# Which step TensorE is handed next: a planner's rule for heads and feed-forward, and the rings of its PSUM banks

## The chip, the cores and the metric

One core of a Trainium2 chip runs the whole program. The time is that of one execution on the device, in microseconds (us); of several runs the median counts. The engines are PE (TensorE, matrix products), DVE (VectorE), ACT (ScalarE), POOL (GpSimd) and SP (SyncE, here a queue of DMA issues). PE writes to PSUM, which has eight banks; each holds 128 x 512 floats.

## The reference

For 8 batches, 8 heads, 576 positions and a head width of 64, block-causal attention is computed; its heads are put side by side to rows of 512; then comes a mixing by a two-dimensional Fourier transform, a normalization and a feed-forward layer of width 2048:

```python
scores = scale * np.matmul(q, k.transpose(0, 1, 3, 2))
scores = np.where(block_i >= block_j, scores, -1000000000.0)   # blocks of 64 positions
attn = softmax(scores)                                          # written out in the reference
x = np.matmul(attn, v)                                          # heads joined: (8, 576, 512)
mixed = np.real(fft(fft(x, axis=1), axis=2))
u = x + mixed
un = (u - mu) / np.sqrt(var + 1e-06)                            # over the 512 of a row
out = u + np.maximum(un @ w_ch1, 0.0) @ w_ch2
```

## The kernel before

**The work.** Products are made of 16-bit halves: each operand is split into a high and a low part, and three of the four cross products are added up. A head (64 of them) goes through PE in stages: four pieces of row maxima (`max_part`, matmuls named ps<-lead with 72 rows; DVE reduces them to M), one `shift` (a transpose of the maxima, ps<-ident,M; ACT makes mt of it, and a DMA of SP's queue writes it into row 72 of "lead"), four pieces of scores (`scores`, ps<-rest and ps<-lead with 73 rows; ACT takes the exponential twice, POOL subtracts to get the low part "pl"), and five steps of values (`values`, av<-VH,ph and the like). These are 14 steps for a head. Two heads share loads and splits of q, k and v.

When the eight heads of a batch are done, its transform follows (`fourier_steps`): a gather through DRAM, folds on DVE and ACT, first stages on PE (ps<-dft,fs), second stages (ps<-dft,zs and ps<-dft,zc), sums on POOL. Then rows of 256 are normalized and turned (`normalized_steps`, ps<-ident,un), and each such group becomes one feed-forward job (`feed_steps`): 18 jobs in all, two for batch 0 and two for batch 1. A job has 64 first-layer steps of three matmuls (h<-uh,W and h<-ul,W) and 32 second-layer steps of three (acc<-W,gh and acc<-W,gl). Job 1 does all of its first layer ahead of its second, because the weights are still being split; later jobs interleave the two layers by pairs of 128 columns.

**The planner.** The order of the instructions on every engine is made when the program is built, by a planner at the end of the kernel. It keeps a clock of its own, `now`, which is PE's; a booked time for each engine; the time at which each finished step is expected to be usable (`done`); and for each pool of PSUM banks a list of the times at which its banks come free (`rings`). A `Step` has a PE cost, a chain of what follows it on other engines (A is ACT, D is DVE, G is POOL, Q is SP's queue, M and L the transfer; every hop adds HOP = 0.3 us), and the keys it comes after. Steps stand in lanes: loads, heads, transforms. The feed-forward steps are a lane of their own; its next step is called `filler`, and `feed` says that it may go. `ready(step)` is the time at which a step's inputs, and a bank where it needs one, are expected.

What is taken next is decided here (lines 1315 to 1323, with MARGIN = 0.3 at line 39):

```python
feed = filler is not None and may(filler)
sure = now - (MARGIN if feed and ready(filler) <= now else 0.0)
soon = [i for i in able if ready(heads[i]) <= sure]
if soon:
    i = min(soon, key=lambda i: heads[i].place)
elif feed and ready(filler) <= now or feed and not able:
    i = None                                        # the feed-forward's step
elif able:
    i = min(able, key=lambda i: ready(heads[i]))
```

So with a ready feed-forward step, a step of the other lanes goes first only if it has been ready for 0.3 us. With no ready step at all, the step of the other lanes that is ready first is taken, even where the feed-forward's would be ready before it.

**Banks.** `ps_av` has one bank; `BANKS = {"ps": 3, "h": 2, "acc": 2}` are the other seven. "h" and "acc" belong to the feed-forward jobs; before the first of these, all seven are lent to everything else (`lent`), later the three of "ps" alone. `rings["ps"]` has three times in the order in which the banks were taken, and the one taken longest ago is always the next.

**Order on the chip.** Every engine executes its instructions in the planner's order; semaphores hold an instruction until its inputs are there and until its bank has been read. The planner's expected times have no power over the chip: where a step was expected too early, PE stands and waits.

Of the kernel before, what the change touches and what calls it, by code (L numbers as in the profile page):

```python
# [19 lines left out]
B, H, S, D = 8, 8, 576, 64  # L20
DM = H * D
FF = 4 * DM
P = 128
NF = FF // P
NK = DM // P
# [10 lines left out]


HOP = 0.3
MARGIN = 0.3
AHEAD = (3.0, 6.0)  # L40
FREE = 0.5
BACKLOG = 3.0
# [4 lines left out]

PSHIFT = 5

BANKS = {"ps": 3, "h": 2, "acc": 2}  # L50

KM = D + 8
KS = KM + 1
# [153 lines left out]
def tile_attn_fourier_ffn(  # L207
# [13 lines left out]
    def mm(*args, **kw):  # L221
        return tc.keep_in_program_order(nc.tensor.matmul(*args, **kw))  # L222
# [44 lines left out]
    def both(h):  # L267

        return half_tiles(h % NB)[0:2]
# [33 lines left out]
    lent = list(BANKS)  # L303


    scratch = {"p": [0.0] * 2, "t": [0.0] * 2, "n": [0.0] * 2}

    def may(step):
        return all(x in done for x in step.after) and all(x in done for x in step.need)
# [391 lines left out]
    def values(h, at):  # L701
        g, hh = divmod(h, 2)
        b, n = divmod(h, H)
        vh, vl = VH[g % 2], VL[g % 2]
        if at == 0:
            avs[h] = ps_av.tile([P, 5, D + 1], F32, name="av")
        av = avs[h]
        c = CHUNKS[at]
        tile_, col = ((0, 0), (1, 0), (2, 0), (2, 320), (1, 448))[c]
        ph, pl = probs[h, tile_]  # L710
        for j in range(c, 5):

# [24 lines left out]
        vector.tensor_scalar(den, av[:, :, D], eps, sc, op0=ALU.add, op1=ALU.mult)  # L737
        rec = work.tile([P, 5], F32, name="rec", bufs=2)
        vector.reciprocal(rec, den)
        vector.tensor_tensor(  # L740
            x[:, :, hh], av[:, :, 0:D], rec.unsqueeze(2).to_broadcast([P, 5, D]), op=ALU.mult
        )
        yield
        if hh == 1:
            ds = slice(D * (n - 1), D * (n + 1))
            sync.dma_start(
                xd[0:512, ds].rearrange("(c p) d -> p c d", p=P), x[:, 0:4].rearrange("p c h d -> p c (h d)")
            )
            sync.dma_start(xd[512:576, ds], x[64:128, 4].rearrange("p h d -> p (h d)"))
            yield  # L750
# [31 lines left out]
        return work.tile([P, 2, DM], F32, name="u", bufs=5)  # L782

    def fourier_steps(b):
        U, X, low, up = [], [], [], []

        def mirror():
            xd = xs.pop(b)
            LL, UU = utile(), utile()
            U.extend((UU[:, 0], UU[:, 1], work.tile([97, DM], F32, name="U2", bufs=1)))  # L790
            X.extend((LL[:, 0], LL[:, 1], work.tile([33, DM], F32, name="X2", bufs=1)))
            low.extend(X[0:2])
            up.extend(U[0:2])
            if b % 2 == 0:
                lefts.append(work.tile([P, DM], F32, name="left", bufs=2))
            U2 = U[2]
            sync.dma_start(X[2], xd[256:289])
# [103 lines left out]
        def stage2_cos(c):  # L901
            na, nb = (128, 128) if c < 2 else (33, 32)
            t = ps_tile()
            i = 0
            ns = slice(P * c, P * c + na)
            for m in range(2):
                for a, w in ((0, 0), (0, 1), (1, 0)):
                    mm(t[0:na, 0:KCOL], z["c", m][:, a, ns], cd[:, m, w], start=(i == 0), stop=False)
                    i += 1
            mm(t[0:na, 0:KCOL], ZT[:, ns], tail, start=False, stop=True)  # L910
            yield
            bs = bss[c]
# [115 lines left out]
    def feed_steps(me, uh, ul, us, stores):  # L1028
# [35 lines left out]
        def second(f, n):  # L1064
            if f == 0:
                acc.append(ps["acc"].tile([P, DM], F32, name="acc"))
            gh, gl = gs[f]
            ns = slice(P * n, P * (n + 1))
            for j, (g_, w) in enumerate(((gh, 0), (gh, 1), (gl, 0))):
                mm(acc[n], g_[:, ns], W[:, NF + f, w], start=(f == 0 and j == 0), stop=(f == NF - 1 and j == 2))  # L1070
            if f == NF - 1:
                yield
                u = us[n]
                vector.scalar_tensor_tensor(u, acc[n], inv_w, u, op0=ALU.mult, op1=ALU.add)
                yield
                stores[n](u)
                yield

        def first_steps(f):
            for part in range(NK):  # L1080
# [150 lines left out]
    def weight_lane(w):  # L1231
# [11 lines left out]
        for j in range(NF):  # L1243
# [10 lines left out]
                lambda: weight_parts(NF * w + j), 0.0, ("A0.73", "p1", "A0.72", "G1.2", "p") if j % 2 else ("A0.73", "X0.75"), (("scale", w), ("w", NF * w + j - 2)), ("w", NF * w + j),  # L1254
            )

    def store(b, c):
        return lambda u: sync.dma_start(out[b, P * c:P * (c + 1)], u)

# [27 lines left out]
    while True:  # L1287
# [29 lines left out]
        soon = [i for i in able if ready(heads[i]) <= sure]  # L1317
        if soon:
            i = min(soon, key=lambda i: heads[i].place)
        elif feed and ready(filler) <= now or feed and not able:  # L1320
            i = None
        elif able:
            i = min(able, key=lambda i: ready(heads[i]))
        elif any(sides):
            w = min((w for w, x in enumerate(sides) if x is not None and may(x)), key=lambda w: ready(sides[w]))
            issue(sides[w])
            sides[w] = next(weights[w], None)
            continue
        elif pending:
            give(pending[0][0])  # L1330
            continue
        else:
            assert filler is None and not any(heads)
            break
        if i is None:
            if len(lent) > 1:
                now = max(now, ready(filler), *rings["h"], *rings["acc"])
                lent = ["ps"]
            issue(filler)
            filler = None  # L1340
        else:
            issue(heads[i])
            heads[i] = next(lanes[i], None)
# [46 lines left out]
```

## Time and profile before

| | |
|---|---|
| median of 3 runs | 1216.81 us (1213.17 to 1217.76) |
| the profiled execution | 1216.37 us, its span 1214.6 us |
| PE busy | 1145.7 us, 94% of the span |
| DVE, ACT, POOL busy | 57%, 47%, 34% |
| mean granted clock of TensorE | 0.983 |
| feed-forward matmuls | h 3456 of 256 columns, acc 1728 of 512 columns |

Busy time of PE is the union of its matmuls' spans, whose ends are modelled: it tells whether PE stood idle, not how fast it went. The granted clock is the share of full speed that TensorE was given; at 0.5 a matmul takes twice as long. In a line of the timeline or of a group the tile written stands left of "<-", the tiles read right of it. All instructions go through the helpers at lines 200, 222 and 225, so it is the tiles' names that tell them apart.

### The profile page before, as it was taken

How to read it: one execution, taken by the hardware profiler on the slowest of the kernel's cores; microseconds unless marked ns; L12 is line 12 of the kernel's file. 1: busy time of each engine (PE TensorE's matmuls, PEld its weight loads, DVE VectorE, ACT ScalarE, POOL GpSimd, SP SyncE). 2: the span in 40 equal slices, each digit the busy share in tenths (PEclk: the TensorE clock that was granted, in tenths of full speed). 3: DMA queues.
4: the chain of work that ended last, by engine and by line, in shares of the span. 5: the costliest groups of instructions: out<-in, count | busy, mean ns of one | idle time of the engine just before them, and what ended most of it. 6: DMA issues, size and time to landing. Idle time of an engine off the chain costs nothing.

```text
span 1214.6 us, 25361 instructions
## 1 busy us (share of the span) xinstructions
PE 1145.7 (94%) x10122; PEld 818.8 (67%) x10122; DVE 691.0 (57%) x1525; ACT 568.6 (47%) x1269; POOL 417.0 (34%) x507
## 2 busy tenths in 40 slices
PE   5777788998999999999999999999999999999998
PEld 4553475676677777777776776777677767766665
DVE  6877887566857656675555565657454424431211
ACT  5656667755556465445554535645552112111100
POOL 4552625444443544254242452335350400300000
PEclk9998899999799999999999999999999999999999
DMA  8775453333424234133234222423230110000000
GB/s 259 238 230 168 143 131 104 98 101 91 124 60 130 69 100 128 59 105 88 78 100 116 60 78 81 143 57 95 61 82 11 43 38 2 23 18 1 18 18 18
DMA packets 66124, 108.23 MB, mean 89 GB/s; under 512 B 9671, under 2 KB 36209, under 8 KB 66006
## 3 DMA queue, kind: packets, MB, share of 16 engines
q1 hardware_dynamic: 58662, 82.25, 24.1%
q10 hardware_dynamic: 4384, 16.78, 4.2%
q0 software_dynamic: 2960, 7.58, 2.2%
q8 instruction: 80, 1.31, 0.5%
q14 instruction: 38, 0.31, 0.1%
HBM read 58.50 MB, written 18.89 MB: 64 GB/s over the span
## 4 chain that ended last, share of the span: by engine, by line
PE 83%; DVE 6%; DMA 5%; POOL 2%; ACT 2%; issue 2%; SPq 0%; DVEq 0%; ACTq 0%; POOLq 0%
PE acc L222 30%; PE h L222 30%; PE ps L222 15%; PE av L222 6%; DMA lead<-mt 2%; DVE W L200 2%; PE ps L225 1%; DVE M L200 1%; DMA lead<-rest 1%; POOL u L200 1%; DMA u<-in_moe_w_ch_dram 1%; POOL pl L200 1%; DMA V<-in_v_dram 0%; ACT p L200 0%; SPq L200 0%
## 5 line engine op out<-in xcount | busy, mean ns | idle before, releaser
L222 PE MATMUL h<-uh,W 128*128 128x256 f16 x2304 | 433.0, 274 | 0.0
L200 POOL TENSOR_TENSOR pl<-p,ph 128x288 f16<-128x288 f32 (+1 forms) x256 | 260.1, 1028 | 356.7 <-ACT p L200 327.4
L222 PEld LDWEIGHTS <-W 128*128 128x128 f16 x3456 | 332.7, 99 | 63.4 <-issue 1.9
L222 PE MATMUL acc<-W,gh 128*128 128x512 f16 x1104 | 328.8, 379 | 0.0
L222 PE MATMUL h<-ul,W 128*128 128x256 f16 x1152 | 315.2, 274 | 0.0
L222 PE MATMUL acc<-W,gl 128*128 128x512 f16 x552 | 209.3, 379 | 0.0
L200 DVE SCALAR_TENSOR_TENSOR gl<-h,gh 128x512 f16<-128x512 f32 x138 | 94.9, 688 | 199.9 <-ACT gh L200 199.6
L200 ACT ACTIVATE gh<-h 128x512 f16<-128x512 f32 x138 | 82.4, 597 | 264.9 <-PE h L222 264.0
L200 DVE TENSOR_REDUCE M<-ps 128x1 fp32r<-128x320 f32 (+3 forms) x293 | 131.0, 483 | 119.2 <-PE ps L222 119.0
L222 PE MATMUL ps<-lead 73*128 73x288 f16 (+7 forms) x708 | 162.8, 293 | 16.7 <-DMA lead<-in_c_masks_dram 6.7
L200 ACT ACTIVATE ph<-ps 128x288 f16<-128x288 f32 (+1 forms) x235 | 119.0, 508 | 99.1 <-PE ps L222 98.2
L222 PEld LDWEIGHTS <-gh 128*128 128x128 f16 x1104 | 102.6, 98 | 83.5 <-issue 3.9
L222 PEld LDWEIGHTS <-ph 128*128 128x128 f16 x1920 | 114.2, 103 | 24.5 <-issue 5.1
L222 PE MATMUL av<-VH,pl 128*128 128x65 f16 x960 | 115.7, 200 | 9.0 <-POOL pl L200 7.0
L200 ACT ACTIVATE p<-ps 128x288 f32<-128x288 f32 (+1 forms) x235 | 118.0, 505 | 2.1 <-POOL pl L200 1.0
L222 PE MATMUL av<-VH,ph 128*128 128x65 f16 x960 | 117.0, 202 | 0.7 <-ACT p L200 0.7
L222 PE MATMUL av<-VL,ph 128*128 128x64 f16 x960 | 116.3, 200 | 0.0
L222 PEld LDWEIGHTS <-pl 128*128 128x128 f16 x960 | 93.8, 102 | 11.2 <-POOL pl L200 8.9
L222 PE MATMUL ps<-rest 128*128 128x320 f16 (+3 forms) x356 | 98.3, 291 | 1.6 <-DVE M L200 1.3
L222 PEld LDWEIGHTS <-gl 128*128 128x128 f16 x552 | 53.8, 97 | 65.6 <-DVE gl L200 0.3
L222 PEld LDWEIGHTS <-lead 73*128 73x128 f16 (+1 forms) x744 | 66.1, 103 | 39.0 <-issue 6.5
L222 PEld LDWEIGHTS <-rest 128*128 128x128 f16 x372 | 38.7, 104 | 30.6 <-issue 11.8
(203 smaller groups left out, 1376.3 us busy)
## 6 DMA issues: line engine op xcount, KB each, us to landing
raw<-in_qk_dram SPq DMA_DIRECT2D x30, 576.0 KB
W<-in_moe_w_ch_dram ACTq DMA_DIRECT2D x14, 1024.0 KB
V<-in_v_dram SPq DMA_DIRECT2D x32, 320.0 KB
rest<-lead SPq DMA_DIRECT2D x64, 144.0 KB
rest<-rest SPq DMA_DIRECT2D x60, 144.0 KB
out_dram<-u SPq DMA_DIRECT2D x32, 256.0 KB
xd<-x SPq DMA_DIRECT2D x30, 256.0 KB
lead<-lead SPq DMA_DIRECT2D x60, 72.0 KB
```

Of the source, the lines that this page charges most:

```text
L200: x = f(*args, **kw)
L222: return tc.keep_in_program_order(nc.tensor.matmul(*args, **kw))
L225: return tc.keep_in_program_order(nc.tensor.transpose(*args, **kw))
```

## The change

- MARGIN goes from 0.3 to -0.2: while a feed-forward step is ready, another lane's step is taken from 0.2 us before it is ready.
- With nothing ready, the feed-forward's step is taken where it is ready no later than any other.
- The three banks of "ps" become three pools of one bank each ("ps", "ps1", "ps2"), each a ring of its own; `FREELY` names them where `lent` was `["ps"]`. The one expected to be free first is taken.
- `avs[h]` is declared as a whole bank and used through a view of its first 325 columns. `mine` keeps a batch's own "left" tile.
- `SEVEN = range(0)` guards new code (another way to do the feed-forward, with its helpers `both`, `straight`, `seven`, `combined`); as the range is empty, none of it is called, and the two new scratch keys "v" and "y" appear in its steps alone.

```diff
-MARGIN = 0.3
+MARGIN = -0.2
...
-BANKS = {"ps": 3, "h": 2, "acc": 2}
+BANKS = {"ps": 1, "ps1": 1, "ps2": 1, "h": 2, "acc": 2}
+FREELY = ["ps", "ps1", "ps2"]
+
+SEVEN = range(0)
...
-    scratch = {"p": [0.0] * 2, "t": [0.0] * 2, "n": [0.0] * 2}
+    scratch = {"v": [0.0], "y": [0.0], "p": [0.0] * 2, "t": [0.0] * 2, "n": [0.0] * 2}
...
-            avs[h] = ps_av.tile([P, 5, D + 1], F32, name="av")
-        av = avs[h]
+            avs[h] = ps_av.tile([P, 512], F32, name="av")
+        av = avs[h][:, 0:5 * (D + 1)].rearrange("p (j n) -> p j n", j=5)
...
             if b % 2 == 0:
                 lefts.append(work.tile([P, DM], F32, name="left", bufs=2))
+            mine.append(lefts[-1])
...
-                sync.dma_start(lefts[-1][at:at + 32], X[2][0:32])
-                sync.dma_start(lefts[-1][at + 32:at + 64], U[2][0:32])
+                sync.dma_start(mine[0][at:at + 32], X[2][0:32])
+                sync.dma_start(mine[0][at + 32:at + 64], U[2][0:32])
...
+        if me in SEVEN:
+            FREELY[:] = ["ps", "ps1"]
...
+            return
...
-        elif feed and ready(filler) <= now or feed and not able:
+        elif feed and ready(filler) <= max(now, min((ready(heads[i]) for i in able), default=ready(filler))):
             i = None
...
-                lent = ["ps"]
+                lent = list(FREELY)
```

More of the change, by code (lines that the diff above doesn't have):

```diff
@@ L784, in fourier_steps @@
     def fourier_steps(b):
-        U, X, low, up = [], [], [], []
+        U, X, low, up, mine = [], [], [], [], []
         def mirror():
@@ L1077, in second, with both @@
                 yield
+        def both(k, part):
+            if part == 0:
+                gs[k] = ps["h"].tile([P, 512], F32, name="h")
+            t = gs[k]
+            i = 0
+            for x in range(2):
+                f = k + x * NF // 2
+                fs = slice(P * (f % NK), P * (f % NK + 1))
+                for w, x_ in ((0, uh), (0, ul), (1, uh)):
+                    mm(
+                        t[:, 2 * P * x:2 * P * (x + 1)], W[:, NK * (f // NK) + part, w, fs], x_[:, part],
+                        start=(part == 0 and i == 0), stop=(part == NK - 1 and i == 5), skip_group_check=True,
+                    )
+                    i += 1
+            if part < NK - 1:
+                return
+            yield
+            g32, s32 = (work.tile([P, 5, 2, D], F32, name=x, bufs=1).rearrange("p c h d -> p (c h d)")[:, 0:4 * P] for x in ("V", "x"))
+            scalar.activation(g32, t, AF.Relu)
+            yield
+            a11, a21, a12, a22 = (g32[:, P * x:P * (x + 1)] for x in range(4))
+            s1, s2, s3, s4 = (s32[:, P * x:P * (x + 1)] for x in range(4))
+            gpsimd.tensor_tensor(s1, a21, a22, op=ALU.add)
+            gpsimd.tensor_tensor(s3, a11, a21, op=ALU.subtract)
+            gpsimd.tensor_tensor(s2, s1, a11, op=ALU.subtract)
+            gpsimd.tensor_tensor(s4, a12, s2, op=ALU.subtract)
+            yield
+            sh = work.tile([P, 4 * P], F16, name=f"ph{1 + k % 2}", bufs=1)
+            sl = work.tile([P, 4 * P], F16, name=f"pl{1 + k % 2}", bufs=1)
+            gs["s", k] = sh, sl
+            scalar.copy(sh, s32)
+            yield
+            vector.tensor_tensor(sl, s32, sh, op=ALU.subtract)
+            yield
@@ new lines, in straight, with seven @@
+        def straight(k):
+            t = gs[k]
+            gh = work.tile([P, 4 * P], F16, name="gh", bufs=2)
+            gl = work.tile([P, 4 * P], F16, name="gl", bufs=2)
+            gs["g", k] = gh, gl
+            scalar.activation(gh, t, AF.Relu)
+            yield
+            vector.scalar_tensor_tensor(gl, t, 0.0, gh, op0=ALU.max, op1=ALU.subtract)
+            yield
+        half = DM // 2
+        def seven(k, which):
+            if not acc:
+                for pool_, name in ((ps["acc"], "acc"), (ps["acc"], "acc"), (ps_av, "av"), (ps["ps2"], "ps2")):
+                    t = pool_.tile([P, DM], F32, name=name)
+                    acc.extend((t[:, 0:half], t[:, half:]))
+            w1, w2 = W[:, NF + k], W[:, NF + k + NF // 2]
+            at = lambda x: slice(P * x, P * (x + 1))
+            g, s_, c = gs["g", k], gs["s", k], COMBINED[k]
+            left, right = slice(0, half), slice(half, DM)
+            table = (
+                (g, 0, lambda x: w1[:, x, left]), (g, 2, lambda x: w2[:, x, left]),
+                (s_, 1, lambda x: c("2", x)), (s_, 2, lambda x: c("3", x)),
+                (s_, 0, lambda x: c("1", x)), (s_, 3, lambda x: w2[:, x, right]),
+                (g, 3, lambda x: c("4", x)),
+            )
+            for i in which:
+                a, x, b = table[i]
+                for j, (y, w) in enumerate(((0, 0), (0, 1), (1, 0))):
+                    mm(
+                        acc[i], a[y][:, at(x)], b(w), start=(k == 0 and j == 0 and i % 2 == 0),
+                        stop=(k == NF // 2 - 1 and j == 2 and (i % 2 == 1 or i == 6)), skip_group_check=True,
+                    )
+            if k < NF // 2 - 1 or which[-1] != 6:
+                return
+            yield
+            u0, u1 = us
+            p1, p2, p3, p4, p5, p6, p7 = acc[0:7]
+            x = work.tile([P, KCOL], F32, name="dif", bufs=1)[:, 0:half]
+            y = work.tile([P, KCOL], F32, name="add", bufs=1)[:, 0:half]
+            scalar.activation(x, p1, AF.Copy, scale=inv_w)
+            yield
+            add = lambda to, p, from_: vector.scalar_tensor_tensor(to, p, inv_w, from_, op0=ALU.mult, op1=ALU.add)
+            c11, c12, c21, c22 = u0[:, left], u0[:, right], u1[:, left], u1[:, right]
+            add(c11, p1, c11)
+            add(x, p3, x)
+            add(y, p4, x)
+            add(c12, p5, c12)
+            add(c12, p6, c12)
+            add(c11, p2, c11)
+            add(c22, p5, c22)
+            add(c21, p7, c21)
+            yield
+            gpsimd.tensor_tensor(c12, c12, x, op=ALU.add)
+            gpsimd.tensor_tensor(c21, c21, y, op=ALU.add)
+            gpsimd.tensor_tensor(c22, c22, y, op=ALU.add)
+            yield
+            stores[0](u0)
+            stores[1](u1)
+            yield
@@ new lines, in both_steps @@
+        def both_steps(k):
+            for part in range(NK):
+                last = part == NK - 1
+                after = ()
+                if part == 0:
+                    after = (("t", me, 0), ("t", me, 1)) + ((("g", me, k - 2),) if k > 1 else ())
+                yield Step(
+                    lambda part=part: both(k, part), 0.654, ("v1", "A0.6", "y1", "G1.8", "v", "A0.6", "X0.72", "y") if last else (), after,
+                    ("s", me, k) if last else None,
+                )
+            yield Step(lambda: straight(k), 0.0, ("A0.6", "D0.72"), (), ("g", me, k))
@@ new lines, in seven_steps @@
+        def seven_steps(k):
+            for which in ((0, 1, 6), (4, 2, 3, 5)) if k < NF // 2 - 1 else ((0, 2, 3, 4), (5, 1, 6)):
+                last = k == NF // 2 - 1 and which[-1] == 6
+                yield Step(
+                    lambda which=which: seven(k, which), 0.327 * len(which),
+                    ("A0.4", "D3.6", "G2.1", "Q1.2") if last else (),
+                    (("s", me, k), ("g", me, k), ("TT", k), ("V", B * H - 1, 4)),
+                    ("F", me) if last else None,
+                )
@@ L1079, in first_steps @@
+        if me in SEVEN:
+            FREELY[:] = ["ps", "ps1"]
+            nk = NF // 2
+            for k in range(nk + 2):
+                if k < nk:
+                    yield from both_steps(k)
+                if k > 1:
+                    yield from seven_steps(k - 2)
+            return
         def first_steps(f):
```

39 lines of the change are left out of this document (added).

## The prediction

> **What bounds the kernel now.** I read the page first: busy times, then the slices.
>
> ```profile
> span 1214.6 us, 25361 instructions
> ...
> PE 1145.7 (94%) x10122; PEld 818.8 (67%) x10122; DVE 691.0 (57%) x1525; ACT 568.6 (47%) x1269; POOL 417.0 (34%) x507
> ...
> PE   5777788998999999999999999999999999999998
> ...
> PEclk9998899999799999999999999999999999999999
> ```
>
> PE is full from about the eighth slice on; its granted clock falls in slices 4, 5 and 11. All PE work has to be done whatever its order, so the end is PE work plus the time that PE loses. The windows view tells where it loses (columns: window, length, busy time and count of PE, PEld, DVE, ACT, POOL, then granted clock, DMA share, GB/s).
>
> ```profile
> 30.40:60.70 30.30, 23.35 (x203) 16.67 (x203) 27.22 (x63) 20.49 (x47) 15.51 (x17) 1.00 0.77 239
> ...
> 151.80:182.20 30.40, 27.08 (x270) 22.16 (x269) 26.22 (x58) 19.65 (x47) 8.70 (x9) 0.93 0.51 131
> 182.20:212.60 30.40, 25.65 (x255) 16.01 (x254) 24.27 (x53) 24.21 (x52) 17.47 (x15) 1.00 0.39 104
> 212.60:242.90 30.30, 29.57 (x314) 20.45 (x313) 17.56 (x46) 22.48 (x49) 15.02 (x15) 1.00 0.34 98
> ...
> 637.70:668.00 30.30, 28.17 (x233) 19.48 (x231) 18.11 (x43) 13.19 (x33) 6.27 (x8) 0.94 0.46 116
> ```
>
> From 151.8 to 242.9 PE idles 3.32 + 4.75 + 0.73 = 8.8 us, with DVE at 26.22 of 30.40 in the first of these windows. The window at 637.7 loses 2.1 us and 0.06 of its clock. The largest loss after that start is in finer windows around 300:
>
> ```profile
> 290.00:300.00 10.00, 8.47 (x98) 6.95 (x96) 8.13 (x14) 4.51 (x12) 7.97 (x11) 1.00 0.75 215
> 300.00:310.00 10.00, 4.67 (x21) 1.78 (x22) 9.72 (x28) 6.20 (x15) 4.78 (x10) 0.63 0.49 145
> 310.00:320.00 10.00, 9.89 (x93) 8.38 (x94) 7.61 (x18) 6.70 (x15) 6.77 (x10) 0.68 0.33 83
> ```
>
> Idle is 1.53 + 5.33 + 0.11 = 6.97 us; the clock takes 0.37 x 4.67 + 0.32 x 9.89 = 4.9 us more: 11.9 us lost in 30. The timeline of PE says why (start, length, then in brackets the idle time before and what ended it):
>
> ```profile
> 290.35 0.38 PE L222 MATMUL acc<-W,gl 128*128 128x512 f16 x1
> ...
> 301.58 0.22 PE L222 MATMUL ps<-ident,M 128*5 128x128 f32 x1 [2.30 <-DVE M L200]
> ...
> 302.76 1.44 PE L222 MATMUL ps<-lead 72*128 72x320 f16 x3 [0.80 <-ACT mt L200]
> ...
> 305.94 0.40 PE L222 MATMUL ps<-lead 73*128 73x288 f16 x1 [1.50 <-DMA lead<-mt]
> ...
> 307.85 0.27 PE L222 MATMUL ps<-ident,M 128*5 128x128 f32 x1 [1.04 <-DVE M L200]
> ...
> 313.31 1.95 PE L225 MATMUL ps<-ident,un 128*128 128x128 f32 x8
> ...
> 316.95 0.27 PE L222 MATMUL h<-uh,W 128*128 128x256 f16 x1
> ```
>
> Between the last "acc" at 290.35 and the next "h" at 316.95 there is no feed-forward step at all, 26 us. The two groups of batch 0 are used up and batch 1's first rows are only turned (ident,un) at 313.3. PE then runs at the pace of single heads: shift, DMA, scores. So the time that counts is how early batch 1 (heads 8 to 15, then its transform) gets through. The chain of waits from 150 to 320, by line:
>
> ```profile
> by line: PE acc L222 19.5%; PE h L222 16.9%; PE ps L222 15.3%; PE av L222 6.8%; DVE M L200 5.5%; DMA u<-in_moe_w_ch_dram 4.9%; DVE W L200 4.2%; SPq L200 2.2%; DVE lead L200 2.1%; DVE pw L200 1.8%; DMA lead<-mt 1.8%; issue 1.6%; DVE rest L20
> ```
>
> Feed-forward steps (acc and h) are 36.4% of it: heads and transform stand behind them in PE's order. That is the order which the change edits.
>
> **The change, part by part.** Feed-forward work starts here:
>
> ```profile
> 150.45 0.37 PE L222 MATMUL h<-uh,W 128*128 128x256 f16 x1
> ```
>
> Both new rules ask for a ready or waiting feed-forward step, so before 150 us only the rings differ.
>
> *MARGIN from 0.3 to -0.2.* While a feed-forward step is ready, a heads' step was taken once it had been ready for 0.3 us; now it is taken up to 0.2 us before. Each such step moves up by about 0.5 us, with all that it issues on ACT, DVE, POOL and SP. What that does to batch 1 I work out from the pace of the heads, one shift (ident,M) each, first without feed-forward work, then with it:
>
> ```profile
> L222 PE MATMUL ps<-ident,M x3: 268/268/402, 31.9 to 71.0; 128*5 128x128 f32 x3
> ...
> L222 PE MATMUL h<-ident,M x2: 267/269/271, 51.0 to 79.6; 128*5 128x128 f32 x2
> ...
> L222 PE MATMUL acc<-ident,M x1: 402/402/402, 40.8 to 40.8; 128*5 128x128 f32 x1
> ```
>
> ```profile
> L222 PE MATMUL ps<-ident,M x7: 221/226/454, 155.4 to 225.6; 128*5 128x128 f32 x7
> ```
>
> Six shifts from 31.9 to 79.6 are 9.5 us a head; seven from 155.4 to 225.6 are 11.7. Sharing PE costs a head 2.2 us. A head has four PE stages one behind the other (maxima, shift, scores, values); 0.5 us off each would be 2 us, but heads overlap by pairs and DVE is nearly full there. I take half of the 2.2: 1 us for each of six heads, 6 us. The transform has PE stages in a row too:
>
> ```profile
> L222 PE MATMUL ps<-dft,fs x33: 290/297/484, 266.5 to 285.3; 128*128 128x290 f32 x12, 128*128 128x288 f32 x12, 128*2 128x290 f32 x4, 98*128 98x290 f32 x2
> ```
>
> Up to 290 four of them stand among feed-forward steps (two first stages, a second-stage pair): 4 x 0.5 = 2 us. Together batch 1 comes 8 us sooner (none if DVE and DMA set the pace, 15 if all 2.2 us and the transform's 2 are won). In those 8 us the heads behind it are ahead as well and take PE from the feed-forward steps: PE would have spent about a third of 8 us on heads, so feed-forward work lasts 2.7 us longer. The hole of 26.4 us shrinks by 10.7 to 15.7. By the rows, the first 15.7 us of it (to 306.4) hold 1.53 + 0.64 x 5.33 = 4.9 us of idle. Of 11.9 us lost, 7.0 are won if the clock holds. I take **-7** (bounds 0 and -11.9).
>
> On the clock: the longest single wait in these rows is 2.30 us, and the clock fell to 0.63. [...]
>
> What the earlier steps cost: those that PE reaches before their input is there. In the long mixed stretch PE waits hardly ever (waits from 334 to 640, then 668 to 1200, each the only row of its answer):
>
> ```profile
> PE ps L222 <- ACT p L200: 0.2, 1, 0.2
> ...
> PE ps L222 <- DVE M L200: 0.6, 1, 0.6
> ```
>
> How much room such a step has, at one of the closest that I read (DVE, PE, SP):
>
> ```profile
> 646.30 0.21 DVE L200 TENSOR_SCALAR M<-M 128x1 fp32r<-128x1 f32 x1
> ...
> 647.26 0.41 PE L222 MATMUL ps<-ident,M 128*5 128x128 f32 x1
> 649.79 0.30 PE L222 MATMUL ps<-lead 72*128 72x64 f16 x3 [2.13 <-DMA lead<-rest]
> ...
> 647.27 2.52 SPq L200 DMA_DIRECT2D lead<-mt  x2
> ```
>
> The maxima are done at 646.51, the shift starts at 647.26: 0.75 us, of which 0.5 goes. The chip's other engines run ahead of the plan, so I take **0** there. The wait of 2.13 us is of another kind: a copy that landed later than planned, on a queue that was late. 0.5 us less room makes such a wait 0.5 longer; another order may drop it or add one. With the clock after it (0.06 x 28.17 = 1.7) it is 3.8 us: bounds -4 and +4, taken 0.
>
> Where DVE is full, heads' steps do wait (waits from 100 to 212):
>
> ```profile
> PE ps L222 <- DVE M L200: 2.8, 3, 2.2
> PE ps L222 <- ACT rest L200: 1.9, 1, 1.9
> PE ps L222 <- DMA lead<-mt: 1.5, 1, 1.5
> ...
> PE ps L222 <- DMA lead<-rest: 0.9, 1, 0.9
> ```
>
> Six waits, each 0.5 us longer at most: +3. Behind a waiting step stands all of PE, and ACT, which takes the next exponentials.
>
> *The feed-forward step where it is ready sooner.* Before, with nothing ready, PE was handed the heads' step that is ready first, though a feed-forward step might be ready before it. Now the sooner one goes first. It can fill part of the 8.8 us idle between 151.8 and 242.9, at most about half, since second-layer weights are still being made then: -4. But it also uses up feed-forward work before the hole. I set it against the +3: **0**, bounds -4 and +3.
>
> *Three rings.* The oldest of the three banks no longer has to be the one taken; the plan picks whichever it believes free first. No wait quoted names a bank as its cause, and before 150 us seven are lent. **0**, bounds -3 and +3. The wider "av" tile fits its one bank, `mine` holds the same tile as before, the two scratch keys and all code behind `SEVEN = range(0)` issue nothing: 0.
>
> Sum: the profiled execution took 1216.4 us (span 1214.6 and 1.8 around it), 0.4 below the median of 1216.81. 1216.4 - 7 = 1209.4; against the median 1209.8. I say **1209.5**. A measurement of this kernel tells about 0.5% (6.1 us) from no change: faster is below 1210.7, slower above 1222.9.
>
> **The rivals.**
> 1. *The hole closes whole.* For: by the upper bound batch 1 is 15 us sooner, and feed-forward work lasts 5 us longer (a third of 15), 20 of 26.4 us. Against: DVE at 9.72 of 10 in the worst window. All of 11.9 goes: 1204.5, and 1200.5 with the -4 of the second rule.
> 2. *The hole shrinks, the half clock stays.* A single wait of 2.13 us sufficed for a fall at 650. Then 6.97 - 4.9 = 2.1 us are won: 1214.3. [...]
> 3. *Batch 1 is paced by DVE and DMA.* DVE 26.22 of 30.40 from 151.8 to 182.2 speaks for it, the chain's 36.4% against it. No gain: 1216.4.
> 4. *Slower: the early steps wait.* If the plan had no room against the chip, PE would stand up to 0.2 us before many heads' steps. Feed-forward steps last 0.33 and 0.65 us by these rows of the chain of waits (24 matmuls are eight steps, 12 are four):
>
> ```profile
> 1174.10 2.59 PE acc L222 x12
> 1176.69 2.62 PE h L222 x24
> ```
>
>    PE's next step is chosen every 0.49 us on average, so 0.2 / 0.49 = 41% of the heads' steps are taken early, at a mean wait of 0.1 us. The heads after 330:
>
> ```profile
> L222 PE MATMUL ps<-ident,M x41: 223/304/411, 337.8 to 901.0; 128*5 128x128 f32 x41
> ```
>
>    41 heads have 14 PE steps each, 574 steps: 574 x 0.41 x 0.1 = 23.5 us, 1232.9 after the gain of 7. It decides from 13 us on, 23 ns a step. Against it stands the 0.75 us of room. [...]
>
> **How the numbers follow.** Forecast 0.34; hole closed 0.22; half clock stays 0.12; paced by DVE 0.15; slower 0.17. My forecast reaches from 1205 to 1214 by the bounds of its small terms, two thirds of it below 1210.7 (0.22, the rest 0.12 "same"). Faster: 0.22 + 0.22 + 0.02 from a lucky order in the third case = 0.46. Same: 0.12 + 0.12 + 0.11 + 0.03 of the slower case that ends small = 0.38. Slower: 0.14 + 0.02 = 0.16. The range is 1199 (hole closed, second rule at its best, a little of the late wait) to 1221 (the first three terms at 0, rings and waits at their worst); about a tenth is left out on each side.
>
> **What would show it.** Right: shifts 155 to 226 closer than 11.7 us; (ident,un) of batch 1 near 305 instead of 313.3; the stretch without h and acc near 16 us; clock 1.00 or nearly so between 300 and 320; the pure feed-forward tail starting sooner, since heads end sooner. Wrong: the same hole with the same clock (rivals 2, 3), or PE waits on DVE M, pl, lead<-mt spread over 334 to 900, which now hold 0.8 us beside the one of 2.13 (rival 4). A shift of the first "h" step away from 150 would mean that the rings matter where I said they don't.

## The result, and the profile after

The changed kernel takes 1233.33 us (median of 4 runs, 1229.55 to 1236.51) where the kernel before takes 1214.99 (4 runs, 1212.65 to 1217.76): a ratio of **1.0146** [1.0111, 1.0181]. It is 1.5% slower. The forecast was 1209.5 us, and the range ended at 1221.

The page of the changed kernel: busy times, then PE and its clock in forty slices.

```profile
span 1234.7 us, 25365 instructions
...
PE 1146.0 (93%) x10122; PEld 817.7 (66%) x10122; DVE 688.4 (56%) x1525; ACT 566.9 (46%) x1269; POOL 417.7 (34%) x507
...
PE   5754797989999999999999999999999999999998
...
PEclk9766896999999999999999999999999999999999
```

PE has the same 10122 matmul records and the same busy time, 1146.0 us against 1145.7. The work did not change, its order did. PE is now lower in slices 3, 4 and 7, and slices 10 and 11, where the hole around 300 stood, are full. (The clock digits of the first slices can't be compared between the two kernels; the last section says why.) Where the time went is read from four windows that cover the span (length, busy time and count of PE, PEld, DVE, ACT, POOL, then clock, DMA share, GB/s), first the kernel before:

```profile
0.00:150.00 150.00, 103.83 (x729) 70.64 (x729) 117.12 (x237) 96.62 (x208) 69.80 (x87) 0.94 0.69 208
150.00:260.00 110.00, 101.21 (x996) 71.61 (x997) 81.03 (x184) 76.15 (x171) 49.47 (x48) 0.97 0.44 122
260.00:350.00 90.00, 83.03 (x800) 60.78 (x799) 58.62 (x137) 49.58 (x115) 38.83 (x49) 0.92 0.28 79
350.00:1214.60 864.60, 857.66 (x7604) 615.75 (x7602) 434.21 (x969) 346.27 (x776) 258.90 (x325) 1.00 0.23 65
```

The same windows of the changed kernel:

```profile
0.00:150.00 150.00, 88.82 (x651) 61.05 (x652) 109.92 (x225) 85.26 (x182) 67.75 (x80) 0.77 0.64 196
150.00:260.00 110.00, 95.31 (x881) 65.25 (x880) 78.61 (x172) 80.25 (x178) 49.88 (x49) 0.86 0.39 109
260.00:350.00 90.00, 86.59 (x836) 63.82 (x834) 60.32 (x143) 48.41 (x112) 35.80 (x47) 1.00 0.35 100
350.00:1234.70 884.70, 875.31 (x7760) 627.56 (x7757) 439.56 (x986) 352.99 (x799) 264.28 (x332) 1.00 0.24 65
```

Idle time of PE is length less busy time. In the first 150 us it rises from 46.2 to 61.2 us (+15.0), from 150 to 260 from 8.8 to 14.7 (+5.9); from 260 to 350 it falls from 7.0 to 3.4 (-3.6), and after 350 it rises by 2.4. Together that is +19.8, and the span grew by 20.1. Busy time is longer where PE runs slower (in the kernel before a values matmul, av<-VH,ph, takes 243 ns from 60 to 70 and 193 from 180 to 190), so the split over the stages is a rough one, but the counts agree: by 150 us 729 matmuls had started before the change, and 651 after it. Read from the other end: at 350 us PE has 875.3 - 857.7 = 17.6 us more work ahead of it. **Most of the loss is there by 150 us, before the first feed-forward step**, where of the three edits only the rings act.

### The profile page after: what moved, and what is told of

The parts are those of the page before. It is cut to its first block, busy times and chain, and to the rows that moved or that the text cites. A ratio compares the mean times of both kernels' runs of the same rounds, so it can differ in the third digit from the quotient of the medians.

```text
span 1234.7 us, 25365 instructions
## 1 busy us (share of the span) xinstructions
PE 1146.0 (93%) x10122; PEld 817.7 (66%) x10122; DVE 688.4 (56%) x1525; ACT 566.9 (46%) x1269; POOL 417.7 (34%) x507
## 4 chain that ended last, share of the span: by engine, by line
PE 78%; DVE 7%; DMA 6%; POOL 3%; ACT 2%; issue 2%; SPq 1%; ACTq 0%; DVEq 0%; POOLq 0%
PE h L225 29%; PE acc L225 28%; PE ps L225 14%; PE av L225 5%; DMA lead<-mt 2%; DVE W L203 2%; DVE M L203 1%; PE ps L228 1%; POOL u L203 1%; SPq L203 1%; DMA lead<-rest 1%; DMA V<-in_v_dram 1%; DVE VL L203 1%; POOL pl L203 1%; POOL U L203 1%
## 5 line engine op out<-in xcount | busy, mean ns | idle before, releaser
L225 PE MATMUL h<-uh,W 128*128 128x256 f16 x2304 | 424.8, 273 | 0.0
L203 POOL TENSOR_TENSOR pl<-p,ph 128x288 f16<-128x288 f32 (+1 forms) x256 | 263.4, 1042 | 382.4 <-ACT p L203 373.2
L225 PE MATMUL ps<-lead 72*128 72x512 f16 (+6 forms) x715 | 165.5, 293 | 29.4 <-DMA lead<-mt 9.0
L203 DVE TENSOR_REDUCE M<-ps 128x2 fp32r<-128x128 f32 (+3 forms) x295 | 132.6, 484 | 100.5 <-PE ps L225 99.9
L203 ACT ACTIVATE ph<-ps 128x288 f16<-128x288 f32 (+1 forms) x240 | 121.5, 508 | 98.9 <-PE ps L225 98.2
L203 ACT ACTIVATE p<-ps 128x288 f32<-128x288 f32 (+1 forms) x240 | 121.0, 507 | 2.8 <-POOL pl L203 2.2
L225 PE MATMUL ps<-rest 128*128 128x192 f16 (+3 forms) x361 | 100.6, 293 | 1.9 <-DVE add L203 1.1
L225 PEld LDWEIGHTS <-lead 73*128 73x128 f16 (+1 forms) x744 | 66.2, 103 | 48.3 <-issue 11.7
```

Of the source, the lines that this page charges most:

```text
L203: x = f(*args, **kw)
```

## The experiments

The kernels below start from the kernel before or from the changed one; all compute the whole output. Ratios are against the kernel before on the same chip, whose median there was 1217.0 to 1218.9 us. Times in the table are us from the start of the span, read from the tiles named.

| | before | after | rings only | both rules | weights late | weights early |
|---|---|---|---|---|---|---|
| its label | | | e1 | e2 | e15 | e14 |
| ratio | 1 | 1.0146 | 1.0118 | 0.9978 | 1.0103 | 1.0097 |
| scale of layer-1 weights (wst,ones) | 86.6 | 112.2 | 110.5 | 86.4 | 101.2 | 83.1 |
| last split of layer-1 weights (W,turns) | 137.7 | 157.1 | 157.2 | 137.5 | 151.7 | 135.2 |
| first scores of head 8 | 137.9 | 157.3 | 157.5 | 137.9 | 152.9 | 135.4 |
| first "h" | 150.4 | 155.2 | 155.4 | 150.2 | 154.5 | 156.6 |
| batch 0's rows turned (ident,un) | 140.9 | 148.6 | 148.6 | 140.6 | 149.3 | 146.0 |
| first second-layer step (acc<-W,gh) | 191.9 | 211.1 | 212.4 | 187.0 | 206.6 | 195.8 |
| heads of batch 1 done (DEN) | 239.5 | 254.1 | 253.9 | 240.7 | 252.6 | 246.1 |
| batch 1's rows turned (ident,un) | 313.3 | 327.6 | 331.0 | 305.4 | 327.4 | 322.3 |

### Which part costs: rings and rules apart

Rings only, on the kernel before:

```diff
-BANKS = {"ps": 3, "h": 2, "acc": 2}
+BANKS = {"ps": 1, "ps1": 1, "ps2": 1, "h": 2, "acc": 2}
+FREELY = ["ps", "ps1", "ps2"]
...
-                lent = ["ps"]
+                lent = list(FREELY)
```

> The kernel before with the three rings alone (MARGIN 0.3 and the old rule kept). Theory R (the rings reorder the steps before 150 us, where PE lost some 10 us, and that delay stays): 1225 to 1234, batch 0's first turned rows near 148 as after, and clock well under 1.00 between 30 and 100. Theory M (MARGIN -0.2 makes PE wait for steps that aren't ready, from 150 on): 1212 to 1218, with the opening of before. Theory P (the planner's order is so touchy that any edit moves the time either way): anything, with no part of the change standing out over the four runs.

Both rules and the old ring, on the kernel before:

```diff
-MARGIN = 0.3
+MARGIN = -0.2
...
-        elif feed and ready(filler) <= now or feed and not able:
+        elif feed and ready(filler) <= max(now, min((ready(heads[i]) for i in able), default=ready(filler))):
```

> The kernel before with both selection rules (MARGIN -0.2, the feed-forward's step where it is ready sooner) and the old ring of three. Theory R: 1205 to 1214, the opening up to 150 as before, the hole without feed-forward steps around 300 shorter than 26 us. Theory M: 1225 to 1234, PE idle for DVE M and DMA lead steps from 150 to 260 as after. Theory P: anything.

One half of this diff each, MARGIN alone and the other line alone:

> The kernel before with MARGIN -0.2 alone. Theory R: 1206 to 1216. Theory M: 1222 to 1232, most of the loss of after. If the two rules need one another, this lies apart from the run with both by over 5 us.

> The kernel before with the rule 'feed-forward's step where it is ready sooner' alone. Theories R and M alike: 1211 to 1218, since with MARGIN 0.3 a feed-forward step is nearly always ready and the new branch is seldom taken. Theory P: moves by more than 5 us.

Measured: rings only 1.0118 [1.0083, 1.0153] (1235.91 us, just above theory R's range); both rules 0.9978 [0.9959, 0.9996] (1216.83, above theory R's range and well below theory M's); MARGIN alone 1.0083 [1.0055, 1.0110] (1229.34); the sooner rule alone 1.0076 [1.0052, 1.0101] (1229.13). The rings alone give nearly the whole loss, 0.0118 x 1218.9 = 14.4 us, and all of the table's shift: down to the last split at 157 the column of e1 is that of the change. The rules together don't hurt. MARGIN alone came out in theory M's range, but with both rules that theory fails. That the two might need one another had been named; that the sooner rule alone would cost 0.8% had not. The redraws below deal with both.

What the rings alter first stands in the timeline of PE (start, length). The kernel before:

```profile
32.47 0.58 PE L222 MATMUL h<-lead 72*128 72x448 f16 x1
32.84 0.26 PE L222 MATMUL av<-VH,ph 128*128 128x65 f16 x1
...
33.68 0.62 PE L222 MATMUL h<-lead 72*128 72x512 f16 x1
```

And the changed kernel at the same place of its order:

```profile
32.96 0.58 PE L225 MATMUL ps<-lead 72*128 72x448 f16 x1
33.33 0.63 PE L225 MATMUL h<-lead 72*128 72x512 f16 x1
33.76 0.26 PE L225 MATMUL av<-VH,ph 128*128 128x65 f16 x1
```

This is the first difference between the two orders, and the same one separates e1 from before. The 72x448 piece goes to a bank of "ps" in place of a lent one of "h", and with an "h" bank still to be had, the next row-maxima piece goes ahead of a values step. No wait stands at these rows in either kernel. The planner expected banks at other times, and decided otherwise from 33 us on.

### Where in time the rings cost

The changed kernel with the old single ring until the first feed-forward step, three rings from then on:

```diff
+        name = current
+        if name == "three":
+            name = turn[0]
+            turn.append(turn.pop(0))
...
-    lent = list(BANKS)
+    rings["three"] = [0.0] * 3
+    turn = list(FREELY)
+    lent = ["three", "h", "acc"]
...
-            if len(lent) > 1:
+            if "three" in lent:
+                for x, r in zip(turn, rings["three"]):
+                    rings[x] = [r]
```

> The changed kernel, but its three banks are taken as one ring, in the order of before, until the first feed-forward step; from there on as three rings, with both new rules. Theory O (what was lost comes from the opening alone: the order of the steps before 150 us delays the first layer's weight scale from 86.6 to 112 and with it the second-layer weights): the scale's matmul back at 86 to 87, first second-layer step near 190 instead of 211, no stretch without feed-forward steps before 211, time 1210 to 1220, as the run with both rules and the old ring or better. Theory L (three rings do harm at any time, by a tighter order): 1226 to 1236, though the opening is that of before.

The same late rings in the kernel before, with the old rules:

> The kernel before with the three rings only from the first feed-forward step on, old rules. Theory O: within 5 us of before (1212 to 1223), 13 us or more under the run with the rings from the start. Theory L: 1230 or more, as that run.

Measured: 1.0028 [1.0008, 1.0047] (1223.1 us) and 1.0068 [1.0049, 1.0088] (1226.63), both between the ranges of the two theories. With the opening's order put back, 1.2 of the 1.5% are gone. In e5 the layer-1 scale is at 87.6 again, the last split at 138.6, the first second-layer step at 188.6. So most of the loss is made in the opening. The rings after the opening are a small loss at most: e6 costs 0.7%, which the next runs show to be within what a mere redraw of the order costs.

### How much an order costs that was changed for nothing

HOP = 0.3 us is the planner's guess of a semaphore's way from engine to engine. It exists in the plan alone; 1 ns more or less changes no instruction, only which of two close steps comes first.

```diff
-HOP = 0.3
+HOP = 0.301
```

> The kernel before with HOP 0.301 instead of 0.3, an edit that means nothing but makes the planner break its ties otherwise from about the first feed-forward step on. It measures how far an order drifts by chance. If each single rule's loss of 0.8% is a cause of its own, this stays within 0.3% of before; if the order after 150 us is a matter of luck (theory P), this moves by 0.4% or more either way, and the single rules' losses can't be told from it.

HOP = 0.299 in the kernel before, then 0.301 and 0.299 in the kernel with both rules (e2):

> The kernel before with HOP 0.299: a second redraw of its order that means nothing. If the order of before is a lucky one among its neighbours: 1.004 to 1.010 of before, like HOP 0.301. If 0.301 was the unlucky one: within 0.2%.

> Both new rules with the old ring (0.998 of before) and HOP 0.301. If the two rules are worth something of their own, this stays under the kernel before with the same HOP (1.007), at 0.995 to 1.002. If 0.998 was luck, 1.004 to 1.010.

> Both new rules with the old ring and HOP 0.299, the second redraw: 0.995 to 1.002 if the rules are worth something, 1.004 to 1.010 if not. Over the three values of HOP the rules' mean against before's mean is what the rules bring; the spread over HOP is what an order costs by chance.

| HOP | kernel before | both rules |
|---|---|---|
| 0.299 | 0.9999 [0.9980, 1.0018] | 0.9968 [0.9952, 0.9984] |
| 0.300 | 1 | 0.9978 [0.9959, 0.9996] |
| 0.301 | 1.0069 [1.0045, 1.0093] | 0.9991 [0.9970, 1.0012] |

One nanosecond in the plan costs 0.7%. **A single order is a draw**: the losses of e3, e4 and e6 (0.7 to 0.8%) can't be told from this, and no cause is claimed for them. The ratios of the two columns don't overlap, though their intervals do; with means of 1.0023 and 0.9979 the rules bring some 0.4% by three draws a side, 0.2% by the pair at 0.300. The rings' 1.2% and the change's 1.5% are more than any redraw showed, but three draws a column don't bound the luck. Nor does any of them reach the opening: in all of these kernels PE's order up to the first feed-forward step is that of the kernel before, and the change and e1 share one other. **What an opening costs by chance was not measured**; if the opening of the kernel before is a lucky one, the runs with rings would look the same. The e13 kernel (1213.66 us) is the fastest of this case.

### What goes wrong in the opening: the weights

The feed-forward weights are loaded, squared and summed for a scale, then split, all in between the heads of batch 0. The planner puts a step of this work in only where its engine is booked no more than AHEAD beyond the moment (3 us, in some cases 6), or where it delays nothing else. ACT's queue issues the fourth weight load so, first in the kernel before, then in the changed one (start, length):

```profile
32.17 0.37 ACTq L200 DMA_DIRECT2D W<-in_moe_w_ch_dram  x1
```

```profile
41.75 0.38 ACTq L203 DMA_DIRECT2D W<-in_moe_w_ch_dram  x1
```

From there the loads fall further behind, from 9.6 us at this one to 24.2 at the eighth, the last of the first layer (95.58 instead of 71.36), and the layer-1 scale is taken at 112.20 instead of 86.6 (groups of the tile wst: count, min/median/max in ns, first and last start). Before:

```profile
L222 PE MATMUL ps<-wst,ones x4: 169/302/353, 86.6 to 186.5; 128*128 128x1 f32 x4
```

After, with the waits of PE from 100 to 150 (total, times, longest) and POOL's timeline in two more fences:

```profile
L225 PE MATMUL ps<-wst,ones x4: 352/362/373, 112.2 to 204.4; 128*128 128x1 f32 x4
```

```profile
PE ps L225 <- DVE wst L203: 11.6, 1, 11.6
```

```profile
108.28 1.00 POOL L203 DMA_INDIRECT U<-xd,rows  x1 [9.36 <-DMA lead<-mt]
...
110.89 0.95 POOL L203 DMA_INDIRECT u<-xd,rows  x1 [0.30 <-issue]
111.83 0.12 POOL L203 MEMSET ul<- 128x1 f32 x1
```

The longest wait of PE in the changed kernel, 11.6 us, ends with DVE's sum of the weights' squares, which waits for a 0.12 us memset, which stands on POOL behind the gather of batch 0. That was the first suspect. In this run DVE zeroes the sum itself:

```diff
-            gpsimd.memset(wsum[:, i + 1:i + 2], 0.0)
+            vector.memset(wsum[:, i + 1:i + 2], 0.0)
```

> The changed kernel, with the small memset of the weight sums issued on DVE instead of POOL (same values). In the trace of after DVE waits 7.3 us and PE 11.6 us because this memset stands on POOL's queue behind the gather of batch 0. Theory O: the scale's matmul near 105 instead of 112, PE's wait of 11.6 us down to 5 or less, first second-layer step some 7 us sooner than 211, time 1224 to 1230. If that queue doesn't matter: the same time as after, 1230 to 1236, with another wait in its place.

Measured 1.0131 [1.0092, 1.0170] (1234.13 us), the change's time. The scale comes 9 us sooner, at 103.2, but the last split only 1.9 (155.2) and the first second-layer step 2.4 (208.7). **The longest wait was not the one that counted.** The theory fell; behind it stood the loads. Their limit is raised, for the whole run and then only until the layer-1 scale is done:

```diff
-AHEAD = (3.0, 6.0)
+AHEAD = (6.0, 9.0)
```

> The changed kernel with AHEAD (6, 9) instead of (3, 6): a step that splits or loads weights may go in where its engine is booked up to 6 (9) us ahead. Theory O': with three rings the heads' steps look ready sooner in the opening, ACT and DVE stand booked further ahead, and the planner turns the weights' steps away by this limit. Then the fourth weight load goes out near 32 instead of 42 us, the first layer's scale is known at 100 or before instead of 112, the first second-layer step is 10 us or more before 211, and the time falls to 1215 to 1228. If something else holds the weights, the scale stays near 112 and the time at 1230 or more.

```diff
-            if ahead <= AHEAD[engine in ("D", "X") and first] or at + ahead + cost + FREE <= until:
+            if ahead <= (AHEAD if ("scale", 0) in done else (6.0, 9.0))[engine in ("D", "X") and first] or at + ahead + cost + FREE <= until:
```

> The changed kernel with AHEAD (6, 9) until the first layer's scale is planned, (3, 6) after it. Theory G (the weights' lateness in the opening passes through the condition of line 1295 to batch 1's heads): last split near 134 to 140 instead of 157, head 8's scores right behind it, head 15 done at 235 to 243 instead of 254, time 1214 to 1224. If the opening's other steps carry the loss: the weights early, but head 15 still at 250 and the time at 1230 or more.

And the other way round, the limit lowered in the kernel before, so that its weights come late:

```diff
-            if ahead <= AHEAD[engine in ("D", "X") and first] or at + ahead + cost + FREE <= until:
+            if ahead <= (AHEAD if ("scale", 0) in done else (2.0, 4.0))[engine in ("D", "X") and first] or at + ahead + cost + FREE <= until:
```

> The kernel before, old ring and old rules, with AHEAD (2, 4) until the first layer's scale is planned, so that the weights go in later in the opening. Theory G: the last split 8 to 25 us later than 137.7, head 15 about as much later than 239.5 less a few us, time 1.005 to 1.015 of before. If lateness of the weights is harmless: within 0.3% of before, or of its neighbours in HOP (0.9999 to 1.007).

Measured: 1.0168 [1.0142, 1.0195], 1.0097 [1.0067, 1.0128] and 1.0103 [1.0076, 1.0130]. In e10 the fourth load is back in its old place:

```profile
32.14 0.37 ACTq L203 DMA_DIRECT2D W<-in_moe_w_ch_dram  x1
```

So the limit held it up, and the stages came as theory O' said (scale at 85.0, first second-layer step at 200.3). The time didn't: 1239.11 us, no faster than the change. As e10 keeps the raised limit for everything later too, the cleaner pair is e14 and e15. The first two windows of e15, the kernel before with late weights:

```profile
0.00:150.00 150.00, 90.53 (x659) 61.88 (x660) 109.86 (x227) 89.45 (x189) 62.81 (x80) 0.81 0.65 200
150.00:260.00 110.00, 97.61 (x933) 68.39 (x933) 79.95 (x175) 75.96 (x170) 43.59 (x46) 0.91 0.38 107
```

And of e14, the changed kernel with early weights:

```profile
0.00:150.00 150.00, 102.06 (x730) 69.84 (x730) 115.60 (x239) 95.92 (x207) 68.79 (x85) 0.78 0.66 207
150.00:260.00 110.00, 97.21 (x958) 68.67 (x959) 74.34 (x168) 76.39 (x170) 49.11 (x51) 0.91 0.41 112
```

Late weights alone, with the old ring and the old rules, raise the idle time of the first 150 us from 46.2 to 59.5 us, put the first second-layer step at 206.6 and batch 1's turn at 327.4, and cost 1.0%: much of the picture of the change, though the hole near 300 stays (26.2 us without feed-forward steps, from 304.8 to 331.0). Early weights bring the idle time of the change's opening from 61.2 down to 47.9, and 730 matmuls have started by 150 us, as many as before. But only a third of the loss comes back (1.5 to 1.0%, with intervals that overlap), and the time, 1230.68 us, is that of the other theory: batch 0's turn is at 146.0 against 140.9 before, batch 1's heads end at 246.1 against 239.5, and the window from 150 to 260 is little better (12.8 us idle, 14.7 in the change).

So late weights move the later stages back as the change does. That they make the loss in time is not shown: 1.0103 is hardly above the 1.0069 of a mere redraw, and early weights won little in e14 and nothing in e10. Every kernel here whose opening is not that of the kernel before costs 1.0% or more, e15 with its one ring too. What in the opening's order costs the time, and how much of it is the luck of the draw, stays open.

### How late weights hold up batch 1

Line 1295 of the kernel before lets the heads of batch 1 start only when the last layer-1 split is done. In the kernel before (timeline of PE):

```profile
137.72 0.38 PE L222 MATMUL ps<-W,turns 128*128 128x512 f16 x1 [2.20 <-ACT W L200]
137.94 0.28 PE L222 MATMUL h<-rest 128*128 128x288 f16 x1
```

In the changed one:

```profile
156.19 1.24 PE L225 MATMUL ps<-W,turns 128*128 128x512 f32 x3
157.27 0.29 PE L225 MATMUL ps<-rest 128*128 128x288 f16 x1
```

Head 8's first scores follow the last split within 0.2 us in both. If the gate were merely in the way, the change without it would win:

```diff
-            if x is not None and may(x) and (i == len(lanes) - 1 or x.place < H or ('w', 15) in done)
+            if x is not None and may(x)
```

> The changed kernel without the condition of line 1295 (heads of batch 1 and later wait in the plan until all first-layer weights are split). Theory G: head 8's scores no longer follow the last split; head 15 is done before 250, time under after by 5 us or more (1218 to 1229). If the heads couldn't have run sooner anyway, since DVE and ACT are busy with the weights: the same time as after within 0.3%.

Measured 1.0288 [1.0251, 1.0325] (1253.16 us), twice the loss. Head 8's scores start at 105.9 and batch 1's heads are done at 228.8, 25 us sooner than in the change, as theory G said. But the splits, now in competition with them, end 66 us later (groups of the tile turns):

```profile
L225 PE MATMUL ps<-W,turns x36: 379/592/1061, 141.4 to 223.2; 128*128 128x512 f32 x24, 128*128 128x512 f16 x12
```

Batch 1's turn comes at 360.1. The gate is worth its wait, and heads that end sooner are not by themselves a gain.

The second-layer weights are late by the same chain (their scale comes at 204.4 instead of 186.5), and that makes a new hole in the changed kernel. First its timeline (last first-layer step of job 1, first second-layer step), then its windows:

```profile
187.35 0.27 PE L225 MATMUL h<-uh,W 128*128 128x256 f16 x1
...
211.09 0.60 PE L225 MATMUL acc<-W,gh 128*128 128x512 f16 x2
```

```profile
190.00:210.00 20.00, 15.15 (x123) 10.71 (x122) 16.40 (x40) 13.34 (x35) 8.10 (x8) 0.51 0.39 112
...
290.00:300.00 10.00, 10.00 (x105) 6.71 (x103) 6.45 (x16) 5.24 (x13) 3.05 (x3) 1.00 0.20 46
300.00:310.00 10.00, 10.00 (x103) 8.78 (x102) 2.83 (x7) 5.03 (x12) 5.39 (x8) 1.00 0.01 2
```

For 23.7 us PE has no feed-forward step to fill in with (5.5 us before, from 186.4 to 191.9); from 190 to 210 it idles 4.85 us and runs at 0.51 of its clock. In exchange it is full from 290 to 310, since the second job of batch 0 now lasts until 329.5 instead of 290.4. **The hole around 300 did not close because batch 1 came sooner: batch 1 came 14 us later, and the feed-forward work was held back by longer.** The hole moved.

## Why the prediction was wrong, step by step

**What bounds the kernel.** Right: the matmuls and their busy time stayed the same, and the span grew with the time that PE lost (19.8 of 20.1 us in the account above).

**Three rings: 0, bounds -3 and +3.** This is the step that failed. It was argued from "No wait quoted names a bank" and from seven banks being lent before 150 us. Both are true, but the one is about waits on the chip and the other about the number of banks. The edit acts in the plan: the time at which it expects a bank decides which step is ready, and that decides the order. The text had said that before 150 us only the rings differ, and that the plan picks the bank it believes free first; it priced the choice as if only a wait on a bank could make it cost. Rings alone measured +14.4 us, nearly five times the upper bound. The sign that had been named for this, the first "h" away from 150, is there: 155.2. Shown is the way from the rings to another order of the opening and from that order to the loss; what in that order costs the time is known only in part.

**MARGIN: -7.** The mechanism is tested by e2, with the second rule and without the rings. (MARGIN alone, e3, shows none of it: a turn at 321.6 and 1.0083, a loss that a redraw can make too.) Batch 1's turn in e2, forecast near 305:

```profile
L225 PE MATMUL ps<-ident,un x16: 273/344/477, 305.4 to 316.0; 128*128 128x128 f32 x16
```

Over the three values of HOP the turn comes at 302.2 to 305.4 with both rules and at 310.2 to 317.0 without, so this is more than one lucky draw. The stretch without feed-forward steps is 17.0 us, from 294.7 to 311.7, forecast 15.7. But the 8 us were won elsewhere than the working said. The shifts of e2, then a transform's second stage in e2:

```profile
L222 PE MATMUL ps<-ident,M x7: 224/303/481, 154.5 to 228.5; 128*5 128x128 f32 x7
```

```profile
L222 PE MATMUL ps<-dft,zc x18: 277/282/467, 284.0 to 291.3; 128*128 128x258 f32 x12, 128*33 128x258 f32 x6
```

And the second stage in the kernel before:

```profile
L222 PE MATMUL ps<-dft,zc x18: 279/282/448, 291.0 to 298.4; 128*128 128x258 f32 x12, 128*33 128x258 f32 x6
```

Seven shifts over 74.0 us are 12.3 us a head, against 11.7 before: the heads were not faster, and batch 1's heads ended at 240.7 (239.5 before). Of the 6 us priced there, none came. The transform, priced at 2 us, brought all of it: its first stages start 3 us sooner (263.5 instead of 266.5), its second stages 7.0, its turn 7.9. Two errors cancelled. For the heads that fits rival 3: something other than PE's order sets their pace. The 2.2 us that sharing PE was to cost a head was also a doubtful figure, since the 9.5 us were read where PE's matmuls took longer (a shift 268 ns against 226 in the rows shown there; the last section has more).

And the smaller hole won little. The windows of e2 there:

```profile
290.00:300.00 10.00, 8.53 (x84) 5.31 (x82) 7.88 (x19) 4.25 (x10) 9.35 (x13) 1.00 0.23 74
300.00:310.00 10.00, 5.40 (x46) 3.79 (x43) 8.38 (x18) 4.91 (x12) 4.18 (x8) 0.73 0.50 131
310.00:320.00 10.00, 9.10 (x79) 7.09 (x79) 5.23 (x11) 6.09 (x15) 4.39 (x7) 0.76 0.20 54
```

Idle time is 1.47 + 4.60 + 0.90 = 6.97 us, as before the change (6.97), and the clock still takes 0.27 x 5.40 + 0.24 x 9.10 = 3.6 us (4.9 before), an estimate from busy time and clock. What a low clock does to PE's pace can be read in the kernel before: from 651.5 to 654.0, at 0.50, first-layer matmuls start 0.214 us apart, from 659.2 to 660.7, at 1.00, 0.109 us apart; their recorded lengths are 421 and 272 ns. The working had cut the idle time in proportion to the hole. It sits in a few waits of PE on single heads and the transform, and these came along: in the timeline of e2 the longest is

```profile
305.33 0.27 PE L222 MATMUL ps<-ident,M 128*5 128x128 f32 x1 [3.05 <-DVE DEN L200]
```

In the window of this wait of 3.05 us the clock reads 0.73; in that of the longest wait before the change, 2.30 us, it reads 0.63. So of -7 there were 1.3 us in this hole. The runs give -0.0022 x 1218.9 = -2.7 us for both rules together [-5.0, -0.5], a little over a third of the forecast's -7 and near rival 2's outcome (-2.1).

**Waits from 150 to 243, the sooner rule: 0.** Idle from 150 to 260 in e2 is 6.4 us against 8.8. The term's bounds (-4 to +4) hold it, but the first 150 us, whose order is the same in e2 and before, differ by as much (43.9 against 46.2), so it isn't a finding.

**Early steps, rival 4: 0 instead of +23.5.** Nearly right. The waits of PE from 334 to 640 in e2 are 2.2 us in all, where they had been 0.2:

```profile
PE ps L222 <- ACT p L200: 0.8, 1, 0.8
PE ps L222 <- DVE add L200: 0.6, 2, 0.4
...
PE acc L222 <- DVE gl L200: 0.2, 1, 0.2
```

So the slack of 0.75 us read at one shift was a fair sample. The time is beyond rival 4's 13 us, but by another mechanism: the rival had the right sign and a wrong place. **Rival 1** had the right picture at 300 for a wrong reason; the price of the hole moving to 190 was in no case.

**The range.** All cases shared the rings at 0, so 1199 to 1221 held the uncertainty of one part alone. That an order made by a planner is a draw (0.7% for 1 ns) was in none of the bounds either.

## What to carry to other kernels

Where a planner writes the order, price an edit by what the planner does with it, not by waits on the chip: a resource no engine waits for can still decide the order, from the first step at which its expected time differs. Before believing a change of under 1% in such a kernel, redraw the order with a neutral change or two of a planner's constant on both sides, and see that the redraw reaches the stage in question. And follow the one-time work (here loads and splits of weights) that gates later stages: the longest wait of PE (11.6 us) was worth nothing when shortened, while weights split 14 us late (e15) moved every later stage up to batch 1's turn by 4 to 15 us.

## What the hardware showed that was not expected

The clock row of the opening does not tell how fast PE ran. Before and e2 have the same order until the first "h"; in their profiled runs the windows from 60 to 70 read, in this order of kernels,

```profile
60.00:70.00 10.00, 6.21 (x62) 4.38 (x61) 9.26 (x13) 5.91 (x17) 5.11 (x5) 1.00 0.83 233
```

```profile
60.00:70.00 10.00, 6.35 (x62) 4.52 (x63) 8.90 (x14) 5.77 (x16) 4.86 (x6) 0.50 1.04 294
```

with a mean clock of 0.98 and 0.61 from 30 to 100. It looks as if half a clock cost nothing: the layer-1 scale comes at 86.6 and 86.4, the last split at 137.7 and 137.5. But the matmuls themselves are equally long. The same values matmuls in these two windows, and then in the kernel before from 180 to 190, where the clock reads 1.00 as well (count, min/median/max in ns):

```profile
L222 PE MATMUL av<-VH,ph x15: 243/243/278, 60.8 to 69.7; 128*128 128x65 f16 x15
```

```profile
L222 PE MATMUL av<-VH,ph x15: 243/245/277, 60.4 to 69.6; 128*128 128x65 f16 x15
```

```profile
L222 PE MATMUL av<-VH,ph x25: 191/193/198, 181.4 to 189.2; 128*128 128x65 f16 x25
```

In both openings a matmul takes 243 to 245 ns, later 193. It takes 243 ns as well in the kernel before from 311.0 to 313.3, where the clock reads 0.50. The clock records of the trace begin at 91 us in the kernel before and at 42 us in e2, and time without a record counts as 1.00 (the window from 30 to 40 reads 1.00 in both kernels). So PE ran slowly in both, and the pair shows nothing on what half a clock costs; the mean clock of 0.983 of the kernel before is too high for the same reason. In the changed kernel the records begin at 40 us, in e1 at 91 us; so theory R's sign of a low clock between 30 and 100 could not be read either (e1's row there says 0.96). Where a clock row reads 1.00 at the start of a trace, compare the lengths of equal matmuls before believing it.
